# A two-layer SiLU kernel: copies out of PSUM on two engines, the first loads on two queues, the last two tiles re-cut

## The chip, the cores and the metric

The kernel runs on one core of a Trainium2 chip. A core has TensorE (PE, matrix products, with its weight loads as PEld), VectorE (DVE), ScalarE (ACT), GpSimd (POOL) and SyncE (SP), and 16 DMA engines that move data between HBM and the core's SBUF. TensorE writes its results to PSUM, from where VectorE or ScalarE fetch them. The metric is the device time of one execution in microseconds (us). A profiled execution has a span besides, from the first to the last instruction.

## The reference

```python
B, S, D, F = 1, 2048, 640, 1728      # all in bf16

def reference(x, w1, w2):            # x [1,S,D], w1 [D,F], w2 [F,D]
    h = jnp.einsum("bsd,df->bsf", x, w1)
    h = jax.nn.silu(h)               # h * sigmoid(h)
    out = jnp.einsum("bsf,fd->bsd", h, w2)
    return out
```

## The kernel before

The kernel is written by hand for each engine: each has its own instruction stream, and all order between engines is made by semaphores. Nothing reorders the work; what stands first in an engine's stream is done first.

D is 5 blocks of 128 (`DT`), F is padded to 14 blocks of 128 (`FT`, the last one half zeros), S is 4 chunks of 512 rows (`NSC`) or 16 tiles of 128 rows (`ST`).

**Head.** x has to stand with D on the partitions (`xT_sb`). For the first chunk of 512 rows this is done on TensorE: SP loads four tiles of 128 rows (L129), TensorE multiplies each of the 20 blocks of 128x128 by an identity (L198, five per tile, into PSUM), and VectorE copies each tile's 640 columns to `xT_sb` (L282). The PSUM places of two tiles are used in turn, so tiles 2 and 3 wait for the copies of tiles 0 and 1 (L195). Ahead of that TensorE does four products on zeros (L184). The other three chunks come by transposing DMAs from SP (L146, five per chunk), which SP begins when the first group of w1 has landed (L151).

**SP's order.** SP issues every transfer: four x tiles; w1 in three groups of 2, 6 and 6 blocks of F (L136); the wait for the first group; the transposing transfers of chunks 1 and 2; w2 in three parts (L155, L158, L164); those of chunk 3; then the 16 stores of output tiles (L173), each after a wait for the copy that made it.

**First product** (L223). For each chunk and each block of F, five matmuls of 128x512 accumulate in one of four PSUM buffers (`ps1`). ScalarE makes the sigmoid of it (L269), VectorE multiplies the two into `hT_sb` (L292). TensorE waits for a w1 group where a block first needs it: the second group at the third block of F (`ft` = 2), the third at `ft` = 8.

**Second product** (L246). For each of 16 tiles of 128 rows and each of the 14 blocks of F, one matmul of 512 columns and one of 128 accumulate in one of two PSUM buffers (`ps2`), both with the same block of `hT_sb` as weights. VectorE copies the 640 columns to one of three output buffers (L305), and SP stores them. TensorE uses a PSUM buffer again when the tile two before it has been copied.

Of the kernel before, what the change touches and what calls it, by code (L numbers as in the profile page):

```python
# [9 lines left out]
def bass_standalone__dense_activation_silu__prompt_kernel(  # L10
# [9 lines left out]
    xf = x.flatten_outer_dims()  # L20
    of = out.flatten_outer_dims()
    S, D = xf.shape
    F = w1.shape[1]
    P = 128
    assert D % P == 0 and S % 512 == 0
    DT = D // P
    FT = (F + P - 1) // P
    FP = FT * P
    F_LAST = F - (FT - 1) * P
    ST = S // P  # L30
    SCH = 512
    NSC = S // SCH
    JB = SCH // P
    NB1 = 4
    NOB = 3
    d_chunks = []
    d0 = 0
    while d0 < D:
        d1 = min(d0 + 512, D)
        d_chunks.append((d0, d1))  # L40
        d0 = d1

    def msz(ft):
        return P

    w1_groups = [(0, 2), (2, 8), (8, FT)]

# [7 lines left out]
    w2_half = n_w2_full // 2  # L55
    n_w2_dmas = 3 if n_w2_full != FT else 2
    N_INIT = 4 if FP != F else 3
    N_WARM_MM = 4

    with ExitStack() as es:  # L60
        def sb(name, shape, dtype):
# [5 lines left out]
        def sem(name):  # L67
            return es.enter_context(nc.semaphore(name))
# [10 lines left out]
        z_sb = sb("z_sb", [P, SCH], bf16)  # L79
        ps1 = ps("ps1", [P, NB1, SCH], fp32)  # L80
        ps2 = ps("ps2", [P, 2, 1024], fp32)
        tp_view = ps2[:, :, :].rearrange("p a (k s) -> p (a k) s", s=P)

        sem_init = sem("sem_init")
        sem_w2pad = sem("sem_w2pad")
        sem_z = sem("sem_z")
        sem_x0 = [sem(f"sem_x0_{j}") for j in range(JB)]
        sem_x = [None] + [sem(f"sem_x{i}") for i in range(1, NSC)]
        sem_w1 = [sem(f"sem_w1_{i}") for i in range(len(w1_groups))]
        sem_w2 = sem("sem_w2")  # L90
        sem_o = [sem(f"sem_o{i}") for i in range(NOB)]
        sem_tp = sem("sem_tp")
        sem_tpc = sem("sem_tpc")
        sem_pe1 = sem("sem_pe1")
        sem_act1 = sem("sem_act1")
        sem_dve1 = sem("sem_dve1")
        sem_pe2 = sem("sem_pe2")
        sem_ev2 = sem("sem_ev2")
        block = es.enter_context(nc.Block())

        w1_v = w1.rearrange("(dt p) f -> p dt f", p=P)
        w2_full_v = w2[0:n_w2_full * P, :].rearrange("(ft p) d -> p ft d", p=P)

        @block.gpsimd
        def _(pool):
# [18 lines left out]

        @block.sync
        def _(sp):
            x0_v = xf[0:SCH, :].rearrange("(j p) d -> p j d", p=P)
            for j in range(JB):
                sp.dma_start(  # L129
                    out=x0_sb[:, j, :], in_=x0_v[:, j, :]  # L130
                ).then_inc(sem_x0[j], 16)

            def load_w1_group(gi):
                a, b = w1_groups[gi]
                f0, f1 = a * P, min(b * P, F)
                sp.dma_start(  # L136
                    out=w1_sb[:, :, f0:f1], in_=w1_v[:, :, f0:f1]
                ).then_inc(sem_w1[gi], 16)

            for gi in range(len(w1_groups)):  # L140
                load_w1_group(gi)

            def x_chunk_transposes(sc):
                s0 = sc * SCH
                for dt in range(DT):
                    sp.dma_start_transpose(  # L146
                        out=xT_sb[:, dt, s0:s0 + SCH],
                        in_=xf[s0:s0 + SCH, dt * P:(dt + 1) * P],
                    ).then_inc(sem_x[sc], 16)

            sp.wait_ge(sem_w1[0], 16)  # L151
            for sc in range(1, NSC):
                x_chunk_transposes(sc)
                if sc == min(2, NSC - 1):
                    sp.dma_start(  # L155
                        out=w2_sb[:, 0:w2_half, :], in_=w2_full_v[:, 0:w2_half, :]
                    ).then_inc(sem_w2, 16)
                    sp.dma_start(  # L158
                        out=w2_sb[:, w2_half:n_w2_full, :],
                        in_=w2_full_v[:, w2_half:n_w2_full, :],  # L160
                    ).then_inc(sem_w2, 16)
                    sp.wait_ge(sem_w2pad, 1)
                    if n_w2_full != FT:
                        sp.dma_start(  # L164
                            out=w2_sb[0:F_LAST, FT - 1, :],
                            in_=w2[n_w2_full * P:F, :],
                        ).then_inc(sem_w2, 16)

            o_cnt = [0] * NOB
            for st in range(ST):  # L170
                ob = st % NOB
                sp.wait_ge(sem_ev2, st + 1)
                sp.dma_start(  # L173
                    out=of[st * P:(st + 1) * P, :], in_=o_sb[:, ob, :]
                ).then_inc(sem_o[ob], 16)
                o_cnt[ob] += 1
            for ob in range(NOB):
                sp.wait_ge(sem_o[ob], 16 * o_cnt[ob])

        @block.tensor  # L180
        def _(pe):
# [8 lines left out]
                )  # L190
            pe.wait_ge(sem_init, N_INIT)
            for j in range(JB):
                pe.wait_ge(sem_x0[j], 16)
                if j >= 2:
                    pe.wait_ge(sem_tpc, j - 1)  # L195
                base = 8 * (j % 2)
                for dt in range(DT):
                    ins = pe.matmul(  # L198
                        tp_view[:, base + dt, :],
                        lhsT=x0_sb[:, j, dt * P:(dt + 1) * P],  # L200
                        rhs=ident[:, :],
                        start=True,
                        stop=True,
                    )
                ins.then_inc(sem_tp, 1)

            w1_waited = set()
            for sc in range(NSC):
                if sc == 0:
                    pe.wait_ge(sem_tpc, JB)  # L210
                else:
                    pe.wait_ge(sem_x[sc], 16 * DT)
                for ft in range(FT):
# [18 lines left out]
            pe.wait_ge(sem_w2pad, 1)  # L232
            pe.wait_ge(sem_w2, 16 * n_w2_dmas)
            dve1_waited = 0
            for st in range(ST):
                b2 = st % 2
                sc = (st * P) // SCH
                if st >= 2:
                    pe.wait_ge(sem_ev2, st - 1)
                for ft in range(FT):  # L240
                    idx = sc * FT + ft
                    if dve1_waited < idx + 1:
                        pe.wait_ge(sem_dve1, idx + 1)
                        dve1_waited = idx + 1
                    for ci, (c0, c1) in enumerate(d_chunks):
                        ins = pe.matmul(  # L246
                            ps2[:, b2, ci * 512:ci * 512 + (c1 - c0)],
                            lhsT=hT_sb[:, ft, st * P:(st + 1) * P],
                            rhs=w2_sb[:, ft, c0:c1],
                            start=(ft == 0),  # L250
                            stop=(ft == FT - 1),
                        )
                ins.then_inc(sem_pe2, 1)

        @block.scalar
        def _(act):
            act.wait_ge(sem_init, N_INIT)
            act.activation(  # L258
                out=warm_sb[:, :], in_=warm_sb[:, :], func=ACT.Sigmoid
            )  # L260
            for sc in range(NSC):
                for ft in range(FT):
                    idx = sc * FT + ft
                    buf = idx % NB1
                    m = msz(ft)
                    act.wait_ge(sem_pe1, idx + 1)
                    if idx >= NB1:
                        act.wait_ge(sem_dve1, idx - NB1 + 1)
                    act.activation(  # L269
                        out=sig_sb[0:m, buf, :],  # L270
                        in_=ps1[0:m, buf, :],
                        func=ACT.Sigmoid,
                    ).then_inc(sem_act1, 1)

        @block.vector
        def _(dve):
            dve.memset(z_sb[:, :], 0.0).then_inc(sem_z, 1)  # L277
            dve.wait_ge(sem_init, N_INIT)
            for j in range(JB):
                base = 8 * (j % 2)  # L280
                dve.wait_ge(sem_tp, j + 1)
                dve.tensor_copy(  # L282
                    out=xT_sb[:, :, j * P:(j + 1) * P],
                    in_=tp_view[:, base:base + DT, :],
                ).then_inc(sem_tpc, 1)
            for sc in range(NSC):
                for ft in range(FT):
                    idx = sc * FT + ft
                    buf = idx % NB1
                    m = msz(ft)  # L290
                    dve.wait_ge(sem_act1, idx + 1)
                    dve.tensor_tensor(  # L292
                        out=hT_sb[0:m, ft, sc * SCH:(sc + 1) * SCH],
                        in0=ps1[0:m, buf, :],
                        in1=sig_sb[0:m, buf, :],
                        op=ALU.mult,
                    ).then_inc(sem_dve1, 1)
            o_cnt = [0] * NOB
            for st in range(ST):
                b2 = st % 2  # L300
                ob = st % NOB
                dve.wait_ge(sem_pe2, st + 1)
                if o_cnt[ob] > 0:
                    dve.wait_ge(sem_o[ob], 16 * o_cnt[ob])
                dve.tensor_copy(  # L305
                    out=o_sb[:, ob, :], in_=ps2[:, b2, 0:D]
                ).then_inc(sem_ev2, 1)
                o_cnt[ob] += 1


# [26 lines left out]
```

## Time and profile before

| | us |
|---|---|
| median of 6 runs | 136.14 |
| lowest, highest of them | 134.98, 137.39 |
| the profiled execution's own time | 135.49 |
| its span | 133.7 |
| TensorE busy in the span | 127.1 (95%) |
| VectorE busy | 55.3 (41%) |
| ScalarE busy | 34.9 (26%) |
| DMA queue of SP, share of the 16 engines | 26.6% |

The time of an execution is 1.8 us longer than its span: start and end lie around it. "Busy" of TensorE counts overlapping matmuls until their modelled ends, so that a mean of 379 ns for a 128x512 matmul is its length and not the distance to the next, which is shorter. The granted clock is TensorE's clock as a share of full speed; over the whole span its mean was 0.987. Ahead of the first recorded change of clock the profile shows 1.00 whatever it was. A time after the name of a wait is the time that the engine stood still before that instruction. L numbers are lines of the kernel as printed above.

### The profile page before, as it was taken

What the parts mean: (1) busy time and instruction counts of PE and PEld (TensorE: products, weight loads), DVE (VectorE), ACT (ScalarE), POOL (GpSimd) and SP (SyncE); (2) the same over time, 40 slices, a digit from 0 to 9 for tenths busy, and PEclk for the clock granted to TensorE, in tenths of its full rate; (3) what the DMA queues carried; (4) which work ended last, traced back from release to release, by engine and by line L of the source; (5) the groups of instructions that cost most, each with busy time, mean ns of one, the idle gap of its engine ahead of it and who ended that gap; (6) DMA issues with size and microseconds to landing.
All of it is one profiled execution on the core that took longest, in us unless ns stands there. A gap on an engine that the chain in (4) does not pass through costs nothing.

```text
span 133.7 us, 1795 instructions
## 1 busy us (share of the span) xinstructions
PE 127.1 (95%) x752; PEld 64.2 (48%) x752; DVE 55.3 (41%) x77; ACT 34.9 (26%) x58; POOL 1.6 (1%) x9
## 2 busy tenths in 40 slices
PE   6579999999999999999999999999999999999990
PEld 2324444444444444444445555555555555555550
DVE  0724666666666666666662222222112222221122
ACT  4004555555555555555550000000000000000000
POOL 4000000000000000000000000000000000000000
PEclk9968999999999999999999999999999999999999
DMA  4999537996000000000000111001111110011111
GB/s 117 268 378 252 112 87 185 381 209 125 0 0 0 2 5 2 0 0 0 0 0 0 54 49 49 18 31 54 49 49 49 49 54 30 19 49 49 52 51 49
DMA packets 14792, 9.78 MB, mean 73 GB/s; under 512 B 8576, under 2 KB 14784, under 8 KB 14784
## 3 DMA queue, kind: packets, MB, share of 16 engines
q1 hardware_dynamic: 14784, 9.67, 26.6%
q8 instruction: 6, 0.10, 0.4%
q14 instruction: 2, 0.02, 0.0%
HBM read 5.08 MB, written 2.62 MB: 58 GB/s over the span
## 4 chain that ended last, share of the span: by engine, by line
PE 92%; DMA 3%; DVE 2%; SPq 1%; issue 0%
PE ps L223 47%; PE ps L246 46%; DMA x_sb<-in_x_dram 3%; DVE xT_sb L282 1%; DVE o_sb L305 1%; SPq L129 1%; PE ps L198 0%
## 5 line engine op out<-in xcount | busy, mean ns | idle before, releaser
L223 PE MATMUL ps<-xT_sb,w_sb 128*128 128x512 bf16 x280 | 62.3, 386 | 1.2 <-DVE xT_sb L282 1.2
L246 PE MATMUL ps<-w_sb,hT_sb 128*128 128x512 bf16 x448 | 61.0, 299 | 0.0
L292 DVE TENSOR_TENSOR hT_sb<-ps,sig_sb 128x512 bf16<-128x512 f32 x56 | 38.7, 691 | 25.0 <-ACT sig_sb L269 25.0
L246 PEld LDWEIGHTS ps<-w_sb,hT_sb 128*128 128x128 bf16 x448 | 34.5, 98 | 26.6
L223 PEld LDWEIGHTS ps<-xT_sb,w_sb 128*128 128x128 bf16 x280 | 27.8, 99 | 35.4 <-issue 2.2
L269 ACT ACTIVATE sig_sb<-ps 128x512 bf16<-128x512 f32 x56 | 33.4, 597 | 34.7 <-PE ps L223 34.7
L305 DVE CAST o_sb<-ps 128x640 bf16<-128x640 f32 x16 | 13.2, 825 | 47.2 <-PE ps L246 47.2
L282 DVE CAST xT_sb<-ps 128x640 bf16<-128x640 f32 x4 | 3.1, 820 | 3.2 <-PE ps L198 3.2
L198 PE MATMUL ps<-ident,x_sb 128*128 128x128 bf16 x20 | 2.1, 261 | 1.2 <-DMA x_sb<-in_x_dram 1.1
L184 PE MATMUL ps<-z_sb 128*128 128x512 bf16 x4 | 1.9, 628 | 1.2 <-DVE z_sb L277 1.2
L198 PEld LDWEIGHTS ps<-ident,x_sb 128*128 128x128 bf16 x20 | 1.6, 118 | 2.4 <-DMA x_sb<-in_x_dram 1.5
L258 ACT ACT_TABLE_LOAD x1 | 1.3, 1283 | 0.7 <-PEq L322 0.7
L184 PEld LDWEIGHTS ps<-z_sb 128*128 128x128 bf16 x4 | 0.4, 132 | 1.7 <-DVE z_sb L277 1.2
L121 POOL MEMSET w_sb<- 128x640 bf16 x1 | 0.6, 631 | 0.0
L277 DVE MEMSET z_sb<- 128x256 uint32 x1 | 0.3, 272 | 0.9 <-PEq L322 0.9
L118 POOL MEMSET w_sb<- 128x320 bf16 x1 | 0.4, 364 | 0.0
L108 POOL TENSOR_SCALAR_AFFINE_SELECT ident<-ident 128x128 bf16<-128x128 bf16 x1 | 0.3, 292 | 0.2 <-POOL ident L106 0.2
L258 ACT ACTIVATE warm_sb<-warm_sb 128x32 f32<-128x32 f32 x1 | 0.2, 229 | 0.0
L106 POOL MEMSET ident<- 128x128 bf16 x1 | 0.2, 204 | 0.3 <-POOLq L322 0.3
L119 POOL MEMSET warm_sb<- 128x32 f32 x1 | 0.1, 124 | 0.0
L322 POOL MEMSET const-bfloat16-1.0<- 128x1 bf16 x1 | 0.1, 101 | 0.0
L322 POOL MEMSET const-uint8-127<- 128x1 uint8 x1 | 0.1, 101 | 0.0
(2 smaller groups left out, 0.2 us busy)
## 6 DMA issues: line engine op xcount, KB each, us to landing
out_dram<-o_sb SPq DMA_DIRECT2D x16, 160.0 KB, 1.8
w_sb<-in_w_dram SPq DMA_DIRECT2D x2, 960.0 KB, 6.1
w_sb<-in_w_dram SPq DMA_DIRECT2D x1, 1120.0 KB, 9.3
w_sb<-in_w_dram SPq DMA_DIRECT2D x1, 880.0 KB, 8.2
x_sb<-in_x_dram SPq DMA_DIRECT2D x4, 160.0 KB, 3.0
w_sb<-in_w_dram SPq DMA_DIRECT2D x1, 320.0 KB, 4.2
xT_sb<-in_x_dram SPq DMA_TRANSPOSE x15, 3.7
w_sb<-in_w_dram SPq DMA_DIRECT2D x1, 80.0 KB, 9.1
```

Of the source, the lines that this page charges most:

```text
L118: pool.memset(w1_sb[:, :, F:FP], 0.0).then_inc(sem_init, 1)
L121: pool.memset(w2_sb[:, FT - 1, :], 0.0).then_inc(sem_w2pad, 1)
L129: sp.dma_start(out=x0_sb[:, j, :], in_=x0_v[:, j, :]).then_inc(sem_x0[j], 16)
L184: pe.matmul(ps1[:, NB1 - 1, :], lhsT=z_sb[:, 0:P], rhs=z_sb[:, :], start=True, stop=True,)
L198: ins = pe.matmul(tp_view[:, base + dt, :], lhsT=x0_sb[:, j, dt * P:(dt + 1) * P], rhs=ident[:, :], start=True, stop=True,)
L223: ins = pe.matmul(ps1[:, buf, :], lhsT=w1_sb[:, dt, ft * P:(ft + 1) * P], rhs=xT_sb[:, dt, sc * SCH:(sc + 1) * SCH], start=(dt == 0), stop ...
L246: ins = pe.matmul(ps2[:, b2, ci * 512:ci * 512 + (c1 - c0)], lhsT=hT_sb[:, ft, st * P:(st + 1) * P], rhs=w2_sb[:, ft, c0:c1], start=(ft == 0),
L258: act.activation(out=warm_sb[:, :], in_=warm_sb[:, :], func=ACT.Sigmoid)
L269: act.activation(out=sig_sb[0:m, buf, :], in_=ps1[0:m, buf, :], func=ACT.Sigmoid,).then_inc(sem_act1, 1)
L282: dve.tensor_copy(out=xT_sb[:, :, j * P:(j + 1) * P], in_=tp_view[:, base:base + DT, :],).then_inc(sem_tpc, 1)
L292: dve.tensor_tensor(out=hT_sb[0:m, ft, sc * SCH:(sc + 1) * SCH], in0=ps1[0:m, buf, :], in1=sig_sb[0:m, buf, :], op=ALU.mult,).then_inc(sem ...
L305: dve.tensor_copy(out=o_sb[:, ob, :], in_=ps2[:, b2, 0:D]).then_inc(sem_ev2, 1)
```

## The change

- The first 512 rows of x are loaded by two transfers of 256 rows (320 KB each), one issued by SP and one by ScalarE. ScalarE then issues the first two groups of w1. SP waits until ScalarE's half of x has landed, issues the third group of w1, then waits for the second group (before: the first) ahead of the transposing transfers.
- TensorE does five products on zeros in place of four. The transposed blocks of the four tiles of the first chunk get four places in PSUM (two in `ps2`, two in `ps1`), so none waits for a copy. VectorE copies two of the five blocks of a tile, ScalarE three; the first product waits for both.
- In the second product, VectorE copies columns 0 to 511 of a tile and ScalarE columns 512 to 639. There are four output buffers in place of three. SP waits for both copies ahead of a store, TensorE for both ahead of using a buffer again.
- Tiles 14 and 15 are done together: first the 512 columns of both (28 matmuls), then the 128 columns of both (28 matmuls). VectorE copies both tiles' 512 columns in one instruction and SP stores them in one transfer; ScalarE copies both tiles' 128 columns in one instruction and stores them itself.

The diff, cut to its core:

```diff
+    NOB = 4
+    DA = 512
+    DB = D - DA
...
-    N_WARM_MM = 4
+    N_WARM_MM = 5
+    TPV = 2
...
+    def tp_slot(j, dt):
+        which = 1 if (j % 4) < 2 else 0
+        base = 8 * (j % 2)
+        slot = base + dt if dt < TPV else base + 4 + (dt - TPV)
+        return which, slot
...
-        tp_view = ps2[:, :, :].rearrange("p a (k s) -> p (a k) s", s=P)
+        tp_views = [
+            ps1[:, :, :].rearrange("p a (k s) -> p (a k) s", s=P),
+            ps2[:, :, :].rearrange("p a (k s) -> p (a k) s", s=P),
+        ]
...
+        segs = []
+        for st in range(ST - 2):
+            b2 = st % 2
+            segs.append([(st, 0, b2, 0, DA), (st, 1, b2, DA, DB)])
+        sA, sB = ST - 2, ST - 1
+        segs.append([(sA, 0, 0, 0, DA), (sB, 0, 0, 512, DA)])
+        segs.append([(sA, 1, 1, 0, DB), (sB, 1, 1, 512, DB)])
...
+        grp_loc = {}
+        for seg in segs:
+            for (st, ci, b2, c0, ncol) in seg:
+                grp_loc[(st, ci)] = (b2, c0, ncol)
...
         @block.sync
         def _(sp):
-            x0_v = xf[0:SCH, :].rearrange("(j p) d -> p j d", p=P)
-            for j in range(JB):
-                sp.dma_start(
-                    out=x0_sb[:, j, :], in_=x0_v[:, j, :]
-                ).then_inc(sem_x0[j], 16)
+            hj = JB // 2
+            sp.dma_start(
+                out=x0_sb[:, 0:hj, :], in_=x0_v[:, 0:hj, :]
+            ).then_inc(sem_x0[0], 16)
...
-            for gi in range(len(w1_groups)):
+            sp.wait_ge(sem_x0[1], 16)
+            for gi in range(2, len(w1_groups)):
                 load_w1_group(gi)
...
-            sp.wait_ge(sem_w1[0], 16)
+            sp.wait_ge(sem_w1[1], 16)
             for sc in range(1, NSC):
                 x_chunk_transposes(sc)
...
-            for st in range(ST):
+            for st in range(ST - 2):
                 ob = st % NOB
-                sp.wait_ge(sem_ev2, st + 1)
+                sp.wait_ge(sem_ev_v, st + 1)
+                sp.wait_ge(sem_ev_a, st + 1)
                 sp.dma_start(
                     out=of[st * P:(st + 1) * P, :], in_=o_sb[:, ob, :]
                 ).then_inc(sem_o[ob], 16)
                 o_cnt[ob] += 1
+            obA = sA % NOB
+            sp.wait_ge(sem_ev_v, ST - 1)
+            sp.dma_start(
+                out=of[sA * P:(sB + 1) * P, 0:DA].rearrange("(t p) c -> p t c", p=P),
+                in_=o_sb[:, obA:obA + 2, 0:DA],
+            ).then_inc(sem_o[obA], 16)
+            o_cnt[obA] += 1
...
             for j in range(JB):
-                pe.wait_ge(sem_x0[j], 16)
-                if j >= 2:
-                    pe.wait_ge(sem_tpc, j - 1)
-                base = 8 * (j % 2)
+                if j % 2 == 0:
+                    pe.wait_ge(sem_x0[j // 2], 16)
+                if j >= 4:
+                    pe.wait_ge(sem_tpc_v, j - 3)
+                    pe.wait_ge(sem_tpc_a, j - 3)
                 for dt in range(DT):
+                    wv, sl = tp_slot(j, dt)
                     ins = pe.matmul(
-                        tp_view[:, base + dt, :],
+                        tp_views[wv][:, sl, :],
                         lhsT=x0_sb[:, j, dt * P:(dt + 1) * P],
                         rhs=ident[:, :],
                         start=True,
...
+            for seg in segs:
+                need = 0
+                for (st, ci, b2, c0, ncol) in seg:
+                    prev = [t for t in buf_users[b2] if t != st]
+                    if prev:
+                        need = max(need, max(prev) + 1)
+                if need > ev_waited:
+                    pe.wait_ge(sem_ev_v, need)
+                    pe.wait_ge(sem_ev_a, need)
+                    ev_waited = need
...
                 for ft in range(FT):
-                    idx = sc * FT + ft
-                    if dve1_waited < idx + 1:
-                        pe.wait_ge(sem_dve1, idx + 1)
-                        dve1_waited = idx + 1
-                    for ci, (c0, c1) in enumerate(d_chunks):
+                    for (st, ci, b2, c0, ncol) in seg:
+                        d0 = 0 if ci == 0 else DA
                         ins = pe.matmul(
-                            ps2[:, b2, ci * 512:ci * 512 + (c1 - c0)],
+                            ps2[:, b2, c0:c0 + ncol],
                             lhsT=hT_sb[:, ft, st * P:(st + 1) * P],
-                            rhs=w2_sb[:, ft, c0:c1],
+                            rhs=w2_sb[:, ft, d0:d0 + ncol],
                             start=(ft == 0),
                             stop=(ft == FT - 1),
                         )
-                ins.then_inc(sem_pe2, 1)
+                        if ft == FT - 1:
+                            ins.then_inc(sem_pe2, 1)
...
         @block.scalar
         def _(act):
+            hj = JB // 2
+            act.dma_start(
+                out=x0_sb[:, hj:JB, :], in_=x0_v[:, hj:JB, :]
+            ).then_inc(sem_x0[1], 16)
+            for gi in range(2):
+                a, b = w1_groups[gi]
+                act.dma_start(
+                    out=w1_sb[:, :, a * P:b * P], in_=w1_v[:, :, a * P:b * P]
+                ).then_inc(sem_w1[gi], 16)
             act.wait_ge(sem_init, N_INIT)
             act.activation(
                 out=warm_sb[:, :], in_=warm_sb[:, :], func=ACT.Sigmoid
             )
+            for j in range(JB):
+                wv, s0_ = tp_slot(j, TPV)
+                act.wait_ge(sem_tp, j + 1)
+                act.copy(
+                    out=xT_sb[:, TPV:DT, j * P:(j + 1) * P],
+                    in_=tp_views[wv][:, s0_:s0_ + (DT - TPV), :],
+                ).then_inc(sem_tpc_a, 1)
...
+            o_cnt = [0] * NOB
+            for st in range(ST - 2):
+                ob = st % NOB
+                b2, c0, ncol = grp_loc[(st, 1)]
+                act.wait_ge(sem_pe2, seg_done_idx[(st, 1)])
+                if o_cnt[ob] > 0:
+                    act.wait_ge(sem_o[ob], 16 * o_cnt[ob])
+                act.copy(
+                    out=o_sb[:, ob, DA:D], in_=ps2[:, b2, c0:c0 + ncol]
+                ).then_inc(sem_ev_a, 1)
+                o_cnt[ob] += 1
...
+            act.wait_ge(sem_pe2, seg_done_idx[(sB, 1)])
...
+            act.copy(
+                out=o_sb[:, obA:obA + 2, DA:D],
+                in_=ps2[:, bA_, cA_:cA_ + 2 * (cB_ - cA_)].rearrange("p (t c) -> p t c", t=2)[:, :, 0:DB],
+            ).then_inc(sem_ev_a, 1)
+            act.wait_ge(sem_ev_a, ST - 1)
+            act.dma_start(
+                out=of[sA * P:(sB + 1) * P, DA:D].rearrange("(t p) c -> p t c", p=P),
+                in_=o_sb[:, obA:obA + 2, DA:D],
+            ).then_inc(sem_ofin, 16)
+            act.wait_ge(sem_ofin, 16)
...
+                wv, s0_ = tp_slot(j, 0)
                 dve.wait_ge(sem_tp, j + 1)
                 dve.tensor_copy(
-                    out=xT_sb[:, :, j * P:(j + 1) * P],
-                    in_=tp_view[:, base:base + DT, :],
-                ).then_inc(sem_tpc, 1)
+                    out=xT_sb[:, 0:TPV, j * P:(j + 1) * P],
+                    in_=tp_views[wv][:, s0_:s0_ + TPV, :],
+                ).then_inc(sem_tpc_v, 1)
...
+            for st in range(ST - 2):
                 ob = st % NOB
-                dve.wait_ge(sem_pe2, st + 1)
+                b2, c0, ncol = grp_loc[(st, 0)]
+                dve.wait_ge(sem_pe2, seg_done_idx[(st, 0)])
                 if o_cnt[ob] > 0:
                     dve.wait_ge(sem_o[ob], 16 * o_cnt[ob])
                 dve.tensor_copy(
-                    out=o_sb[:, ob, :], in_=ps2[:, b2, 0:D]
-                ).then_inc(sem_ev2, 1)
+                    out=o_sb[:, ob, 0:DA], in_=ps2[:, b2, c0:c0 + ncol]
+                ).then_inc(sem_ev_v, 1)
                 o_cnt[ob] += 1
...
+            dve.wait_ge(sem_pe2, seg_done_idx[(sB, 0)])
...
+            dve.tensor_copy(
+                out=o_sb[:, obA:obA + 2, 0:DA],
+                in_=ps2[:, bA_, 0:2 * DA].rearrange("p (t c) -> p t c", t=2),
+            ).then_inc(sem_ev_v, 1)
```

## The prediction

> **What bounds the kernel now.** I read the chain of work that ended last first, because it says where each microsecond of the span lies.
>
> ```profile
> 0.74 0.39 SPq L129
> ...
> 1.20 0.42 SPq L129
> ...
> 1.66 3.69 DMA x_sb<-in_x_dram
> 5.36 0.04 issue
> 5.40 0.47 PE ps L198 x5
> 5.87 0.02 issue
> 5.89 1.57 DVE xT_sb L282 x2
> 7.46 0.05 issue
> 7.50 62.29 PE ps L223 x280
> 69.80 60.87 PE ps L246 x448
> 130.66 0.02 issue
> 130.69 0.82 DVE o_sb L305
> ```
>
> (Start, length, what.) Between 7.50 and 130.66 us TensorE runs without a gap: 123.2 of 133.7 us. No edit touches the number or the widths of those matmuls, so only three things can move: the 7.50 us head, the half-speed stretch inside the first product, and the tail, 133.7 - 130.66 = 3.04 us, of which 0.82 is VectorE's last copy and 2.19 the last store and the end of the program.
>
> Next the table of stretches, for the head and for the clock.
>
> ```profile
> 4.00:5.00 1.00, 0.31 (x4) 0.09 (x1) 1.00 (x2) 0.00 (x0) 0.00 (x0) 1.00 0.85 230
> 5.00:6.00 1.00, 0.56 (x7) 0.40 (x8) 0.61 (x2) 0.00 (x0) 0.00 (x0) 1.00 1.07 310
> 6.00:7.00 1.00, 0.34 (x5) 0.17 (x3) 1.00 (x2) 0.00 (x0) 0.00 (x0) 1.00 1.04 333
> 7.00:8.00 1.00, 0.50 (x2) 0.23 (x3) 0.45 (x1) 0.00 (x0) 0.00 (x0) 0.77 1.04 364
> 8.00:9.00 1.00, 1.00 (x4) 0.36 (x3) 0.00 (x0) 0.00 (x0) 0.00 (x0) 0.50 1.03 369
> ```
>
> (Stretch, its length, busy us of PE, PEld, DVE, ACT, POOL, granted clock, DMA share, GB/s.) The transfer engines are full (0.85 to 1.07) while PE waits for x: the head is bound by bytes, not by who issues them. The clock column falls to 0.50 at 7.54 and, by a finer table, is back at 0.98 from 10.95. So the first product starts at half speed. Warm tiles follow each other by 1.08 us (sigmoids at 12.64, 13.72, 14.79), or 0.216 per matmul; 280 of those are 60.4 us against the 62.29 measured. The half-speed stretch accounts for (10.95 - 7.54) / 2 = 1.7 of that 1.9.
>
> Last, the rows that give prices:
>
> ```profile
> L246 PE MATMUL ps<-w_sb,hT_sb 128*128 128x512 bf16 x224 | 61.0, 379 | 0.0
> L246 PE MATMUL ps<-w_sb,hT_sb 128*128 128x128 bf16 x224 | 49.1, 219 | 0.0
> L269 ACT ACTIVATE sig_sb<-ps 128x512 bf16<-128x512 f32 x56 | 33.4, 597 | 34.7 <-PE ps L223 34.7
> L305 DVE CAST o_sb<-ps 128x640 bf16<-128x640 f32 x16 | 13.2, 825 | 47.2 <-PE ps L246 47.2
> L282 DVE CAST xT_sb<-ps 128x640 bf16<-128x640 f32 x4 | 3.1, 820 | 3.2 <-PE ps L198 3.2
> ```
>
> **The change, part by part.**
>
> *x loads on two queues.* Four SP issues of 160 KB (0.39 to 0.43 us each) become one of 320 KB on SP and one on ACT, both from about 0.74; ACT's first real work is not due before transposes exist, so its issues and its 1.28 us table load lie in the shadow. But the same 640 KB must come through the same engines. By the stretches before (19 KB to 2.0 us, then 310, 203, 230 per us) they have moved 640 KB at about 4.5 us; the fourth tile, by its transposes, was only usable at 5.87. When the two halves share the engines, both land near the end: earliest about 4.5, latest 5.85 as the fourth tile today; I take T = 5.2. What is lost is that the first ten transposes and two copies, done by 5.50 today, now start only at T.
>
> *Transposes and copies.* Behind T come five transposes (0.47, chain) and then four ACT copies of three blocks. The trace has no ScalarE copy; nearest are its sigmoids, 597 ns for 512 columns and 229 for 32 (L258, at 2.03 us). Between them lie 368 ns for 480 columns, 0.77 each, so I take 597 - 128 x 0.77, about 500 ns, for 384; VectorE's pairs (1.57 for two of 0.82) show successive copies overlapping by 0.08. So T + 0.47 + 3 x 0.42 + 0.50 + 0.05 (issue, chain) = T + 2.28. Today it is the third tile's 5.36 + 2.14 = 7.50, with two 0.82 copies. VectorE's share, 256 columns, is at most 0.42 each and lies beside ACT's. The buffer wait before transposes three and four goes, and none takes its place: four tiles have four places. First matmul: 5.2 + 2.28 = 7.48 in place of 7.50, gain 0.02. Bounds: 6.8 for T = 4.5; 8.1 when the transposes run at half clock: twenty spaced 0.107 (today's first ten took 1.18 us), 2.14 + 0.2 to drain + 0.50 + 0.05 = 2.9 after T. The fifth warm-up matmul (0.43) ends at about 3.5, before T: nothing on the path, only activity.
>
> *Clock.* The Trainium skill's page "TensorE: Matmul & The Clock Gate", section "Part 1: The HAM clock gate", says that activity is judged in free-running windows of about 3.4 us, so that what a start pays varies from run to run. The row here: half clock for 3.41 us, after a stretch of the same length (4.13 to 7.54) with PE busy for 1.12 us, and full after one with 2.88. By the row taken alone the changed kernel loses the same 1.7; by the rule anything from 0 to more than that, before and after. Twenty transposes now lie in the last 3.4 us before the stream, where ten did, which leans to a gain. The trace doesn't show how much activity suffices (between 1.12 and 2.88 of 3.4), so I take no gain and keep 0 and 1.7 as ends.
>
> *First-layer weights.* The first two groups (320, 960 KB) move to ACT's queue right behind x; the third (880 KB, SP) waits for ACT's x half, and behind that wait on SP stand it, all 15 transposing transfers, w2 and the stores. Today the second group is issued at 3.08 and takes 6.5 us: 9.6, due at 11.36 (7.50 + ten matmuls at half speed to within one, 3.86). Now the third's packets start about 1.0 us after T, when some 1,200 KB have moved, so about 715 KB of the second are left; with two queues sharing about 370 GB/s evenly they take 3.9 us: 10.1 plus 0.35 for the receipt gives about 10.5. Ends: 9.6 (no sharing) and 11.85 (all 2,800 KB through, today's landing of the third). It is due at 7.48 + 2.16 + 1.70 = 11.34: no stall. If the clock were full at once it would be due at 9.6 and TensorE would stall to 10.5. So the second group also caps what a warmer clock can give: 11.36 - 10.5 = 0.86.
>
> *Transposing transfers* start at the second group's landing (10.5) instead of 6.78. Chunk 1 is five issues of 1.3 us, 17.0, plus up to 3.7 to land: about 20.7, due at 11.3 + 12 x 1.08 = 24.3. Covered with 3.6 us; each microsecond beyond that is one of TensorE. Chunks 2 and 3 and w2 are then up to 4 us later with 15 us or more in hand.
>
> *Second product.* VectorE now copies 512 columns (at most 0.69, as L292 has it), ACT 128 (about 0.28), both far below the 3.80 us that a tile takes on TensorE (60.87 / 16). The second semaphore wait per tile and the extra increments are met long before; 0, and at worst 16 x 0.05 = 0.8.
>
> *Tail.* The last two tiles are re-cut: 28 matmuls of 512, then 28 of 128. Same widths, but the 128s stand together, each with its weight load (98 ns a record, 128 columns). The trace says 60.87 / 224 = 0.272 per pair, less 0.216: 0.056 for a 128. The Trainium skill's TensorE page named above, section "Back-to-back issue gap", has about 81 ns for N=128 in a stream of loads and matmuls. That speaks against the change: 28 x 0.025 = +0.70. Five transposes, also 128 wide with a load each, took 0.47 of which 0.22 is the last one's own length: 0.06 apart. So I take 0.056 and nothing, and keep +0.70 as the end. After the last matmul ACT copies 256 columns, 597 - 256 x 0.77 = 0.40, in place of 0.82, and issues its own 64 KB store; I add 0.1 for its wait on itself and for 256-byte rows: 0.82 - 0.50 = 0.32 gained. VectorE's 1,024 columns (at most 1.32) start 28 x 0.056 = 1.57 us earlier, so SP's 256 KB leave 0.25 before the last matmul ends and have 0.7 us in hand over ACT's store.
>
> **Sum** against the profiled execution (span 133.7, its own time 135.49): head -0.02, clock 0, weights 0, second product 0, tail -0.32: -0.34. The median of the runs is 136.14, 0.65 above the profiled execution, which I take for other clock phases and later landings that both kernels have. 136.14 - 0.34 = 135.8.
>
> **Rivals.** *A warmer clock* (0.23). The denser transposes keep the full clock until the second weight group stops the stream at 10.5: -0.86 - 0.32 = -1.2, 134.9; with x at 4.5 (the third group then starts, and shares, earlier, so the stop stays) hardly more, but runs like the median, 0.65 colder than the profiled one, would gain up to 1.9: 134.3. For it: 20 against 10 transposes; against it: they take only 1.1 us of 3.4 at full clock, as much as the 1.12 that did not suffice.
> *The second weight group becomes the wait* (0.12, the slower side). It lands only at 11.85 while the clock is full at the start: matmul eleven, due 9.6, waits 2.2 us, and the gate takes that for idleness: another 3.4 us at half speed, 1.7. Against 11.36: +0.49 + 1.7 - 0.32 = +1.87, 138.0. It decides once the stop leaves TensorE no busier than in the stretch that was throttled, 1.12 of 3.4 us. For it: two queues with equal claims; against it: half the group is through by then at the rates shown.
> *The change doesn't do what it says* (0.20). Copies by two engines save nothing as T comes at 5.85 or the transposes are cold (8.1 or 8.75 less the shorter half-speed stretch: about +0.5), and the short matmuls cost up to 0.70: 0.5 + 0.35 (half of 0.70) - 0.32 = +0.5, 136.7.
>
> **How the numbers follow.** The likeliest (0.45) has 135.3 to 136.3 of its own. The middle of the range must reach the two middling rivals: 134.3 to 137.0 leaves out most of the stall rival and the far end of the clock's. About 1% is what a measurement of this kernel can tell from no change: below 134.8 lies more than half of the first rival and a little of the likeliest, 0.20; above 137.5 the stall rival and a little of the last, 0.14; between them 0.66.
>
> **What would show it.** First matmul of the first product between 7.1 and 7.8 with ACT's copies of the transposed x as what released it; the clock at 0.5 for about 3.4 us around there; no wait of TensorE for w1, and the second group landing between 10 and 11; the 28 short matmuls 56 ns apart; 2.7 us from the last matmul to the end. A stream that begins before 6.8, or a stop of TensorE for weights, would make the prediction wrong.

## The result and the profile after

| | before | after |
|---|---|---|
| median of the runs | 135.61 us (20 runs, 134.98 to 137.39) | 134.76 us (10 runs, 133.72 to 135.34) |
| ratio | | 0.993, 95% interval 0.990 to 0.996 |
| profiled execution, its span | 135.49, 133.7 | 134.95, 133.1 |
| last matmul to the end of the span | 3.04 | 2.57 |

The change is 0.7% faster (0.4 to 1.0%). A ratio leaves out runs more than 1.5% above the fastest of the same kernel, so it can differ from the quotient of the medians.

The chain of work that ended last, in the changed kernel (start, length, what):

```profile
0.74 3.77 DMA x_sb<-in_x_dram
4.51 0.14 issue
4.64 2.31 PE ps L240 x20
6.95 0.02 issue
6.97 0.44 DVE xT_sb L384
7.41 0.14 issue
7.55 62.14 PE ps L266 x280
69.69 60.87 PE ps L303 x448
130.56 0.02 issue
130.58 0.37 ACT o_sb L366
```

The first product starts at 7.55 us where it started at 7.50, and takes 62.14 where it took 62.29. The second product takes 60.87 as before. The tail, from the last matmul to the end, is 133.13 - 130.56 = 2.57 (here with the spans to two places: 133.13, and 133.70 before). Of the 0.57 us that the span is shorter, 0.47 lie behind the last matmul and 0.10 ahead of it.

The 20 transposes take 2.31 us, 0.107 each: half clock. The clock column says 1.00 there and in all the first 10.7 us, because ahead of the first recorded change it says 1.00 whatever is granted. The spacing of the first product's weight loads tells the truth (0.43 us is half speed, as in the stretch that the kernel before records at 0.50; 0.216 is full speed):

```profile
7.93 0.15 PEld L266 LDWEIGHTS ps<-xT_sb,w_sb 128*128 128x128 bf16 x1 [0.28 <-issue]
8.36 0.15 PEld L266 LDWEIGHTS ps<-xT_sb,w_sb 128*128 128x128 bf16 x1 [0.28 <-issue]
8.79 0.15 PEld L266 LDWEIGHTS ps<-xT_sb,w_sb 128*128 128x128 bf16 x1 [0.28 <-issue]
```

The full clock is first recorded at 10.71. The kernel before has its clock changes at 4.12, 7.54 and 10.95, each 3.41 us after the last by the trace's records of the clock, so I count back from a recorded change in windows of that length. The table of stretches shows how busy TensorE was in the two windows ahead of the one in which the clock woke (columns as in the prediction), and, in the lines below them, in the two windows of the kernel before:

```profile
3.89:7.30 3.41, 2.29 (x20) 2.05 (x20) 1.60 (x4) 1.77 (x5) 0.00 (x0) 1.00 1.06 350
0.48:3.89 3.41, 2.32 (x5) 0.59 (x5) 0.27 (x1) 1.51 (x2) 1.43 (x5) 1.00 0.55 169
...
4.13:7.54 3.41, 1.12 (x14) 0.60 (x12) 2.92 (x4) 0.00 (x0) 0.00 (x0) 1.00 1.00 306
0.71:4.13 3.42, 2.88 (x14) 1.42 (x14) 0.46 (x2) 1.51 (x2) 1.43 (x5) 1.00 0.63 164
```

2.29 and 2.32 us of PE (busy as the profile counts it, to the modelled ends) did not wake the clock. In the kernel before, 2.88 had woken it, and a window with 1.12 had put it back to half. Nor could another place of the windows have helped here: TensorE has nothing to do from 3.50 to 4.64, and no stretch of 3.41 us ahead of the first product holds more than 2.32 us of PE.

The groups that are new:

```profile
L406 DVE CAST o_sb<-ps 128x512 bf16<-128x512 f32 x14 | 9.7, 692 | 42.9 <-PE ps L303 42.9
L354 ACT CAST o_sb<-ps 128x128 bf16<-128x128 f32 x14 | 3.7, 266 | 49.2 <-PE ps L303 49.2
L384 DVE CAST xT_sb<-ps 128x256 bf16<-128x256 f32 x4 | 1.7, 425 | 4.6 <-PE ps L240 4.3
L418 DVE CAST o_sb<-ps 128x1024 bf16<-128x1024 f32 x1 | 1.2, 1225 | 5.4 <-PE ps L303 5.4
L366 ACT CAST o_sb<-ps 128x256 bf16<-128x256 f32 x1 | 0.4, 373 | 7.3 <-PE ps L303 7.3
L331 ACT CAST xT_sb<-ps 128x384 bf16<-128x384 f32 x4 | 1.9, 479 | 1.6 <-PE ps L240 1.5
```

In the steady second product both copying engines stand idle before nearly every copy, waiting for TensorE, so dividing that work there can gain nothing. What counts is the end (the timeline):

```profile
129.02 1.23 DVE L418 CAST o_sb<-ps 128x1024 bf16<-128x1024 f32 x1 [5.35 <-PE ps L303]
130.27 0.38 SPq L212 DMA_DIRECT2D out_dram<-o_sb  x1
130.58 0.37 ACT L366 CAST o_sb<-ps 128x256 bf16<-128x256 f32 x1 [7.34 <-PE ps L303]
130.98 0.39 ACTq L371 DMA_DIRECT2D out_dram<-o_sb  x1
```

VectorE's large copy starts at 129.02 and ends at 130.24, before the last matmul does; only 256 columns on ScalarE and a small store lie behind it. The 28 short matmuls lie between 128.8 and 130.56 and start 56 ns apart.

### The profile page after: what moved, and what is told of

It reads as the page before. It is cut to its first block, busy times and chain, and to the rows that moved or that the text cites. A ratio compares the mean times of both kernels' runs of the same rounds, so it can differ in the third digit from the quotient of the medians.

```text
span 133.1 us, 1847 instructions
## 1 busy us (share of the span) xinstructions
PE 127.6 (96%) x753; PEld 64.8 (49%) x753; DVE 51.6 (39%) x76; ACT 41.0 (31%) x77; POOL 1.6 (1%) x9
## 4 chain that ended last, share of the span: by engine, by line
PE 94%; DMA 3%; DVE 0%; issue 0%; ACT 0%
PE ps L266 47%; PE ps L303 46%; DMA x_sb<-in_x_dram 3%; PE ps L240 2%; DVE xT_sb L384 0%; ACT o_sb L366 0%
## 5 line engine op out<-in xcount | busy, mean ns | idle before, releaser
L303 PE MATMUL ps<-w_sb,hT_sb 128*128 128x512 bf16 (+1 forms) x448 | 61.0, 299 | 0.0
L406 DVE CAST o_sb<-ps 128x512 bf16<-128x512 f32 x14 | 9.7, 692 | 42.9 <-PE ps L303 42.9
L354 ACT CAST o_sb<-ps 128x128 bf16<-128x128 f32 x14 | 3.7, 266 | 49.2 <-PE ps L303 49.2
L384 DVE CAST xT_sb<-ps 128x256 bf16<-128x256 f32 x4 | 1.7, 425 | 4.6 <-PE ps L240 4.3
L418 DVE CAST o_sb<-ps 128x1024 bf16<-128x1024 f32 x1 | 1.2, 1225 | 5.4 <-PE ps L303 5.4
L240 PEld LDWEIGHTS ps<-ident,x_sb 128*128 128x128 bf16 x20 | 2.1, 143 | 2.0 <-issue 2.0
L331 ACT CAST xT_sb<-ps 128x384 bf16<-128x384 f32 x4 | 1.9, 479 | 1.6 <-PE ps L240 1.5
```

The costliest lines, as they stand in the source:

```text
L240: ins = pe.matmul(tp_views[wv][:, sl, :], lhsT=x0_sb[:, j, dt * P:(dt + 1) * P], rhs=ident[:, :], start=True, stop=True,)
L303: ins = pe.matmul(ps2[:, b2, c0:c0 + ncol], lhsT=hT_sb[:, ft, st * P:(st + 1) * P], rhs=w2_sb[:, ft, d0:d0 + ncol], start=(ft == 0), stop= ...
L331: act.copy(out=xT_sb[:, TPV:DT, j * P:(j + 1) * P], in_=tp_views[wv][:, s0_:s0_ + (DT - TPV), :],).then_inc(sem_tpc_a, 1)
L354: act.copy(out=o_sb[:, ob, DA:D], in_=ps2[:, b2, c0:c0 + ncol]).then_inc(sem_ev_a, 1)
L384: dve.tensor_copy(out=xT_sb[:, 0:TPV, j * P:(j + 1) * P], in_=tp_views[wv][:, s0_:s0_ + TPV, :],).then_inc(sem_tpc_v, 1)
L406: dve.tensor_copy(out=o_sb[:, ob, 0:DA], in_=ps2[:, b2, c0:c0 + ncol]).then_inc(sem_ev_v, 1)
```

## Experiments

Theory A: the tail gained, and the head gained nothing because its clock stayed at half. Theory B: the head's gain in clock made the median better. Then, the clock itself: what sets it, and what the head of the change is worth when it is out of the way.

### The two halves of the change apart

e1 is the changed kernel with the head of before; e2 has the head of the change and the second product of before (d_chunks, one copy of 640 columns, one store per tile).

> The head of before (four x loads on SP, VectorE alone copies the transposed x, four warm-up products), the second product of the changed kernel (two engines copy, the last two tiles re-cut). Theory A, the tail is what gained: from the last matmul to the end of the span 2.5 us in place of 3.04, and 0.4 to 0.5 us off the time of before. Theory B, the gain of the median is the head's (it meets the clock more favourably): within 0.2 us of before.

> The head of the changed kernel, the second product of before (VectorE alone copies 640 columns, SP stores each tile). Theory A: the first product starts at 7.5 us as in before, the tail is 3.04 us as in before, and the time is within 0.3 us of before. Theory B: 0.4 us or more below before, with a median nearer to the lowest run.

e1: 135.31 us against 135.41, ratio 1.001 (0.993 to 1.009). e2: 135.24, ratio 1.003 (0.998 to 1.007). The medians cannot tell either half from nothing, so by the time alone neither theory is shown. The traces speak for A: from the last matmul to the end 131.38 - 128.82 = 2.56 us in e1 and 133.78 - 130.73 = 3.05 in e2; and e2's first product starts at 7.44 (before: 7.50). Why the medians are so blunt is seen in e1's profiled execution. It was e1's fastest run (133.21; the others lie between 134.67 and 136.33), its clock was full from 4.75 us on, and its first product began at 7.02 and then stopped for weights:

```profile
3.07 6.39 DMA w_sb<-in_w_dram
9.46 0.05 issue
9.51 3.41 PE ps L250 x15
```

The kernel before has the same two groups: of its 29 runs on that chip six lie at 133.4 to 133.8 and the other 23 at 134.9 to 136.5. That the six are those that met the full clock early is my reading; there is no trace of them. The gap of 1.1 us in one and the same program is larger than what the change does.

### TensorE kept busy in the head

e3, on the changed kernel, and e4, on the kernel before (the edits written short):

```diff
 # e3
-    N_WARM_MM = 5
+    N_WARM_MM = 8
...
                 ins.then_inc(sem_tp, 1)
+            pe.wait_ge(sem_tpc_v, 1)
+            for i in range(6):
+                pe.matmul(ps2[:, 0, 0:P], lhsT=z_sb[:, 0:P], rhs=z_sb[:, 0:P], start=True, stop=True)
 # e4
                 ins.then_inc(sem_tp, 1)
+                if j in (1, 3):
+                    for i in range(10):
+                        pe.matmul(ps1[:, NB1 - 1, 0:P], lhsT=z_sb[:, 0:P], rhs=z_sb[:, 0:P], start=True, stop=True)
```

> The changed kernel with eight products on zeros ahead of the transposes in place of five, and six products of 128 columns on zeros behind them, so that TensorE has hardly a gap between 1.2 us and the first product. If the half clock of the head is set by how much of a 3.4 us stretch TensorE was busy (67 and 68% did not wake it in the changed kernel, 84% did in before), the clock is full before the first product or at most 0.5 us into it, the transposes run 56 ns apart, and the time falls by 1.0 to 2.2 us against the changed kernel (132.6 to 133.8). If the start of the first product itself is what wakes the clock 3.4 us later, nothing moves: 134.8.

> The kernel before with ten products of 128 columns on zeros behind the second and behind the fourth tile's transposes, in gaps where TensorE waited, and nothing else changed. Clock set by busy share: the half-speed stretch of up to 3.4 us in the first product goes or shrinks, and the time falls by 0.8 to 1.8 us against before without any of the change. Otherwise within 0.2 us of before.

e3: 132.89 us (132.65 to 133.35), ratio to before 0.986 (0.980 to 0.992). e4: 133.90 (133.41 to 134.57), ratio 0.992 (0.989 to 0.996). Products that compute nothing, in gaps where TensorE waited, are worth as much on the old kernel as the whole change (0.993), and the scatter shrinks too. In e3 the clock was full from 4.95; the timeline shows the transposes ending 0.9 us sooner and the first product beginning at 6.97:

```profile
4.57 1.47 PE L241 MATMUL ps<-ident,x_sb 128*128 128x128 bf16 x20
5.88 0.50 PE L251 MATMUL ps<-z_sb 128*128 128x128 bf16 x6
```

e8 leaves the six short products of e3 out (eight ahead, none behind).

> The changed kernel with eight products on zeros ahead of the transposes in place of five, and nothing behind them. TensorE is then busy from 1.2 to 4.6 us, for a whole 3.4 us stretch, but idle again for 0.6 to 1 us in the stretch before the first product. If one busy stretch is enough to go to full clock and a stretch with more than about 68% busy to stay there: most runs near e3 (132.9 to 133.5), some at 134.5 that fall back to half clock as before did. If the fill behind the transposes was what mattered: like the changed kernel, 134.8.

133.09 us (132.70 to 133.34), within 0.3 of e3: a busy first window is enough, and none of the six has the time of a run that fell back. Its two windows:

```profile
0.97:4.38 3.41, 3.19 (x8) 1.04 (x8) 0.16 (x1) 1.51 (x2) 1.23 (x4) 1.00 0.69 214
4.38:7.79 3.41, 2.45 (x26) 1.60 (x26) 1.42 (x4) 1.63 (x4) 0.00 (x0) 1.00 1.06 347
```

The closest cases on either side are in e2, whose clock stayed at half after the first of these windows, and in e9 (below), whose clock stayed full after the second:

```profile
4.35:7.76 3.41, 2.61 (x21) 2.19 (x22) 1.70 (x4) 1.91 (x4) 0.00 (x0) 1.00 1.06 350
...
5.94:9.35 3.41, 1.85 (x21) 1.23 (x20) 1.10 (x3) 1.24 (x3) 0.00 (x0) 1.00 1.08 368
```

Over all traces, per window of 3.41 us: at half clock, 2.29, 2.32 and in e2 2.32 and 2.61 us of PE did not wake it; 2.88 (before), 2.97 (e1), 3.19 (e8), 3.23 (e4) and more did. Once awake it stayed so after 1.85 (e9), 2.01 (e1) and 2.45 (e8), and fell after 1.12 (before). So waking takes something between 76 and 84% of a window here, and staying awake something between 33 and 54%.

Where the windows lie is not in the kernel's hands. In seven traces TensorE is busy without a gap from 1.19 us until the clock wakes, by the same eight products and the transposes behind them, and still it woke at 4.38 (e8), 4.52 (e11), 4.94, 4.95, 5.12, 5.72 and 5.94 (e9). That can explain the scatter, by an estimate from the traces. In the profiled execution of the changed kernel, every stretch of 3.41 us that ends at 8.05 or later holds at least 2.79 us of PE (4.64 to 8.05, for one). If that much is enough, the wake falls anywhere from 8.05 to 11.46. Each microsecond of half clock in the first product costs half of one, so the time (134.95 in the profiled execution, with the wake at 10.71) would lie between 133.6 and 135.3; its ten runs lie between 133.72 and 135.34. For e2 the same sum gives 133.9 to 135.6, and its runs lie between 134.09 and 135.56. The ranges fit, but no run was made to test this.

### The tail, with the clock out of the way

e5 is e4 with the second product and tail of the change; e6 is e3 with tiles 14 and 15 done like all others (two engines copy, nothing re-cut); e12 is e3 with the second product of before.

> The kernel of e4 (before, its head filled with products on zeros) with the second product and tail of the changed kernel. With the clock out of the way the tail should be seen in the median: theory A (tail gains) 0.5 us below e4, so about 133.4 where e4 had 133.9; if the tail is worth nothing in the time outside the profile, 133.9.

> The kernel of e3 (changed kernel, head filled) with tiles 14 and 15 done like the others: two engines still copy, SP stores whole tiles, nothing is re-cut. After the last matmul VectorE copies 512 columns (0.69) in place of ScalarE's 0.37 for 256. If it is the re-cut that gains: 0.3 us above e3 (133.2), 2.9 us from the last matmul to the end. If the split of the copies does: as e3 (132.9).

> The head of the changed kernel filled as in e3, with the second product of before. If the second product and tail of the change are worth the 0.5 us that the traces show: 0.5 us above e3 and its repeat, 133.3 to 133.4, with 3.04 us from the last matmul to the end, and as e6 without the re-cut (133.5). The head of the change, the clock out of the way, is then worth the difference to e4: 0.5 us (133.9). If the head is worth nothing: 133.9.

| | median, runs | ratio to before | last matmul to the end |
|---|---|---|---|
| e3, and again as e11 | 132.89 and 132.80 | 0.986 and 0.985 | 2.57 |
| e6, no re-cut | 133.55 (133.25 to 133.71) | 0.986 (0.982 to 0.990) | 2.98 |
| e12, old second product | 133.49 (133.06 to 133.83) | 0.988 (0.984 to 0.993) | 3.05 |
| e4, old head and tail | 133.90 | 0.992 | 3.04 |
| e5, old head, new tail | 133.69 (133.41 to 134.75) | 0.989 (0.984 to 0.994) | 2.56 |

The chains end so in e3, e6 and e12:

```profile
128.45 0.37 ACT o_sb L376
...
128.50 0.69 DVE o_sb L389
...
128.53 0.82 DVE o_sb L364
```

e6 and e12 are alike, 0.6 to 0.7 us above e3: the re-cut of the last two tiles carries the gain of the second product, and dividing the copies between two engines gives nothing by itself that the medians show (0.07 us in the traces). The ratios of e6 and e12 overlap with that of e3, and so do single runs (e3 reaches up to 133.35, e6 down to 133.25, e12 to 133.06), so this rests on the medians and on 0.4 to 0.5 us in the traces. e5 was a miss, 0.2 us below e4 and not 0.5: in its profiled execution the tail was as short as e3's, but the second w1 group landed at 10.19 us (9.22 in e4), and TensorE stood still for it. Between the medians of e12 and e4, which differ in the head and its fillers alone, lie 0.4 us; but the intervals of their ratios overlap, their profiled executions have spans of 131.56 and 131.62, and the first product starts at 7.05 in e12 and at 6.97 in e4. So a gain from the head of the change is not shown, with the clock out of the way either.

> The kernel of e3 once more, on the chip of e9 and e10, to compare them with: the ratio to before within 0.5% of e3's 0.986.

132.80 us, ratio 0.985 (0.980 to 0.990).

### The loads of the head

e7 issues both halves of x and the three w1 groups from SP, without a wait between; e9 is e3 without this line:

```diff
-            sp.wait_ge(sem_x0[1], 16)
             for gi in range(2, len(w1_groups)):
```

> The kernel of e3 with all loads of the head issued by SP: both halves of x, then the three w1 groups, with no wait between. Bytes bind, not the queues: x lands within 0.3 us of e3's 4.4 and 4.8, the time is within 0.2 us of e3. If the second queue helps, 0.4 us or more above e3.

> The kernel of e3 without SP's wait for ScalarE's half of x ahead of the third w1 group, so that its 880 KB compete with x and the first two groups from about 2 us on. If two queues share the engines evenly, the second group lands between 10.5 and 11.8 us in place of 8.7, TensorE stops for it at the third block of the first product for 1.5 us or more, and the time is 1.5 to 2.5 us above e3. If the order of issue still decides, within 0.3 us of e3.

e7: x landed at 3.89 and 4.78 (e3: 4.42 and 4.78), so the second queue does not bring x sooner. The time was nevertheless 133.32, 0.4 to 0.5 above e3 and e11, because the second w1 group landed at 9.60 in place of 8.74 and TensorE stopped for it. (The ratio, 0.985 with 0.981 to 0.989, does not tell e7 from them; the traces do, with spans of 131.5 against 131.0 and 130.9.) e9: 134.58, and twelve runs of which eleven lie between 134.43 and 134.67, 1.8 above e11. Chain of e9:

```profile
1.79 9.06 DMA w_sb<-in_w_dram
10.85 0.05 issue
10.89 1.25 PE ps L275 x5
```

The clock of e9 was full from 5.94, and still the kernel was as slow as the unfilled one: the first group landed at 8.31 (5.77 in e3) and the second at 10.85, after the third, 7.91. The long stop was not where I expected it, at the third block, but ahead of the first matmul, which waited for the first group and began at 8.45 in place of 6.97 (us waited in total, times, longest):

```profile
PE ps L275 <- DMA w_sb<-in_w_dram: 1.6, 1, 1.6
```

The second group then added 0.3 us; it alone would have set the same end, as the chain shows. So two queues let a transfer that isn't urgent overtake one that is, and it is SP's wait that keeps the change from paying for it.

### A version better than both

e10: e3 with x in four loads (tiles 0 and 2 from SP, 1 and 3 from ScalarE), transposed as they land, five products on zeros ahead in place of eight, and smaller first groups of w1.

```diff
-    w1_groups = [(0, 2), (2, 8), (8, FT)]
+    w1_groups = [(0, 2), (2, 4), (4, 8), (8, FT)]
```

> The kernel of e3 with x in four loads (tiles 0 and 2 from SP, 1 and 3 from ScalarE), transposed as they land, five products on zeros ahead and six short ones behind, and w1 in groups of 2, 2, 4 and 6 blocks (ScalarE issues the first two). Nothing is left out. If TensorE's head is now bound by the copies behind the last x tile, the first product starts at about 6.0 us in place of 6.97 and the time is 0.7 to 1.0 us below e3. If the loads bind (the first w1 group at 5.8, the second at 8.7): within 0.3 us of e3.

132.44 us (132.04 to 132.99), ratio 0.982 (0.977 to 0.986): 2% faster than before by the medians (135.34 there), and 0.36 below e11, half of what I expected; the two intervals overlap. The chain tells what is missing:

```profile
3.51 0.14 issue
3.65 2.29 PE ps L240 x20
5.94 0.59 PE ps L250 x6
6.53 0.02 issue
6.55 4.05 PE ps L275 x18
```

With only five products ahead, the clock woke at 6.35, so the transposes took 2.29 us (1.47 in e3). The six fillers behind them cost nothing, though the chain names them: ScalarE's last copy ended at 6.45, and the first weight load came 0.07 us after it, as in e3 (6.87 and 6.94).

## Why the prediction was right, and where it was not

The forecast of 135.8 us had a gain of 0.34; the runs gave 0.85 between the medians (0.5 to 1.4 by the interval of the ratio). A small gain was the right call, and the tail was the right place. The other 0.5 us of the difference to 135.8 is the kernel before, whose median came out at 135.61 with more runs, not 136.14. The median of 134.76 lies within the range, but outside the 135.3 to 136.3 that the likeliest case had for itself, and 0.04 below the 134.8 under which the forecast saw a chance of 0.20. By the number alone the warmer clock (134.9) did better; the trace has the opposite, half clock up to 10.71. So part of the hit is luck. Step by step:

- **x lands at 5.2.** It was usable at 4.64. The byte count of the same paragraph had said 4.5; I moved it up for the late fourth tile (5.85), which was one execution's: in e1, e4 and e5, with the loads of before, that tile landed at 5.05, 5.23 and 5.35, and the third, 5.36 in the kernel before, at 4.6, 4.7 and 4.6.
- **T + 2.28 to the first matmul.** This step failed: it was T + 2.91, the bound given for transposes at half clock (2.9). I had taken full clock because the last ten transposes of before had it. Behind x in one lump they came after 2.32 us of activity in a window, not 2.88. The two errors, -0.6 and +0.6, cancel by luck: 7.55 against the forecast 7.48. ScalarE's copy, 479 ns against 500, was sized well, and it was the last to end (7.45, VectorE's 7.40) and released the first product, 0.07 us later; the chain names VectorE's.
- **Clock: no gain, the same 1.7 us.** Right for the profiled run, with (10.71 - 7.55) / 2 = 1.6. But that "1.12 and 2.88" left the threshold open hid the largest thing to be had in the head: e3 lies 1.9 us below the changed kernel by the medians.
- **The second w1 group at 10.5.** It landed at 8.94, ahead of the 10 to 11 that I had named as a sign. I let the third group's packets start 1.0 us after x; they came 2.46 us after their issue (4.93 to 7.39), and shared only the end. Sharing is real, and dear where the wait is missing (e9: 10.85, 1.8 us). That is about the rival's +1.87, but by another path: in e9 TensorE waited for the first group too, and the clock stayed full. In the change itself the rival could not decide, as it has the wait and a cold clock. The second group does bound a warm kernel (e1, e5, e7).
- **Transposing transfers.** Begun at 8.96, chunk 1 landed at 17.93, due at 24: covered, as forecast.
- **Second product 0.** Right: 60.87 and 60.87.
- **Tail 0.32.** 0.47. The copy took 0.37 (0.40 assumed), and the 0.1 for ScalarE's wait on itself and for short rows was not needed: from the end of its copy to the end of the span it is 2.18 us against 2.19 before.
- **Short matmuls.** 56 ns by the trace against about 81 by the Trainium skill's page "TensorE: Matmul & The Clock Gate", section "Back-to-back issue gap": measured 56 ns from start to start, 28 in a row. The row was right.

What stays open: the traces show 0.6 us, the medians 0.85, and the interval holds both. Whether the head of the change gains the rest by meeting the clock more often could not be settled (e2's interval reaches from -0.2 to +0.7%). Nor was it found why the second w1 group lands later when SP queues all groups at once (9.22 to 10.19 us in e1, e4, e5 and e7, 8.74 to 9.03 in the filled kernels with two queues and the wait). In part other bytes come with it: by the packets, about 430 KB of the third group had moved in e7 when the second landed, and about 330 in e3. But the engines were also slower for a while, 195 GB/s from 5 to 6 us in e7 and 326 in e3.

## What to carry to other kernels

When a kernel starts cold, count TensorE's busy time in every stretch of 3.4 us before the real work, as nobody knows where a window begins: here products on zeros in the gaps were worth more than every edit to copies and queues. Dividing copies between engines that wait for TensorE gives nothing in the steady state; what pays is to arrange that the least copying and storing is left behind the last matmul. A second DMA queue did not bring x sooner and let loads overtake each other, so hold back what isn't due.

## What the runs showed of the hardware

- The wake of the clock needs between 2.61 and 2.88 us of PE in a window of 3.41 (e2, before); 1.85 was enough to keep it (e9), 1.12 was not (before).
- The windows do not begin with the kernel: with TensorE busy from 1.19 us on, the clock woke between 4.38 (e8) and 5.94 us (e9).
- In the profile a clock of 1.00 ahead of the first recorded change means nothing; matmuls 0.43 us apart at 512 columns show half speed there.
- With the other queue full, a transfer's first packet came 2.46 us after its issue (the third w1 group, changed kernel).
- ScalarE copies fp32 from PSUM to bf16 in 266 ns (128 columns), 373 (256) and 479 (384): 0.83 per column and 160; VectorE in 425 (256), 692 (512) and 1225 (1,024).
